# Attention and bilinear feed-forward block: the raw query weights land in XT3's place, and later tiles and PSUM banks take other places

## The chip, the cores and the metric

The kernel runs on one core of one Trainium2 chip. The metric is the device time of one execution in microseconds (us), the median of several runs. A profile is one further execution; its span goes from the first to the last instruction.

## What is computed

One transformer block on 2048 tokens of width 576, in float32:

```python
# 32 query heads of width 18, one shared key head and one shared value head
h  = x + softmax(q k^T / sqrt(18)) v @ wo        # q, k, v from layernorm(x) @ wq, wk, wv
h2 = h + ((n @ w_gate) * (n @ w_up)) @ w_down    # n = layernorm(h); 4608 hidden columns
```

## The kernel before

The tokens are worked in four blocks of 512 (`NB` = 4). Matrix products keep their precision by splitting one or both operands into a high part and a remainder, so a product is two or three matmuls.

**The opening** is `keys_values`. It loads the tokens and the raw weights, normalises each block, turns it over with TensorE transposes (`turns`), and splits the result into the tile `XT[b]` (`parts`: ScalarE writes the high part, VectorE the remainder). From `XT[b]` come the keys (`project`, `keys`), the values and, for block 0, the queries (`query`). The raw query weights come as four pieces of seven heads, `wqr0` to `wqr3`. ScalarE or GpSimd writes their high part to `wq_h` (`highs`, L276), GpSimd the remainder to `wq_l` (`lows`, L279); nothing reads a raw piece after that. The last piece is split by `highs(3, pool.tensor_copy)` and `lows(3)`, and the last block is written to `XT[3]` by the `parts()` behind `turns(3)`. `scale` works out the factors of the normalisation for some chunks of 128 tokens, and leaves minus mean times factor in a small tile `n` (L183).

**The rest.** After the opening, attention of block 0 runs with the queries of blocks 1 to 3 between (`queries`, L445). From about 360 us on the feed-forward of a block (`ffn`, gate and up products at L986, down products in `down` at L946) runs with the attention of a later block between its matmuls: `pair` issues scores (L593) and exponentials (L594), `flush` the sums over the values (L598). From about 1822 us only the last feed-forward work is left.

**What sets the order.** The order of each engine's instructions is the order in which the code issues them (`manual_schedule`). A tile pool gives every tile a place in SBUF (SBUF tiles of one tag share `bufs` slots, as large as the largest tile of the tag), and the layer below adds the semaphore waits that the slots need: who writes to a slot waits for the readers of the tile that was there. The pools lie one behind the other, in the order in which they are opened: `const`, `ln`, `resid`, `q`, `P`, `o`, `oT`, `w0`, then `p0q` (`wq_h`, `wq_l`, `kvq`, `XT0` to `XT3`) and `qb`; after the opening `w`, `hid` and `P2` take the room of `p0q` and `qb`. PSUM has eight banks: tag `s` has four of them (two tiles of two), `f` two, `m` and `a` one each, given out in the order in which the tags are first used.

Before the change the pieces `wqr1` to `wqr3` stand in the three slots of tag `wo_r` of pool `w0` (L145), which the output weights `wo_r` of block 0 use much later (`load_wo_0`, L714 to L716). The first tile in PSUM is `warm` of tag `a` (L305), into which 24 transposes run while the first tokens come in.

Of the kernel before, what the change touches and what calls it, by code (L numbers as in the profile page):

```python
# [17 lines left out]
F32 = mybir.dt.float32  # L18
F32R = mybir.dt.float32r
# [6 lines left out]
P = 128  # L26
S, D, H, DH, F = 2048, 576, 32, 18, 4608
TB = 512
NB = S // TB
NQ = TB // P  # L30
# [24 lines left out]
class Block:  # L55
# [78 lines left out]
    def keys_values(self, others):  # L134
# [7 lines left out]
        wkr = self.qp.tile([P, 5, 6 * DH], F32, tag="q", name="wkr")  # L142
        cols = [(slice(None), slice(None), slice(h0 * DH, (h0 + n) * DH)) for h0, n in QT]
        wqr = [self.qp.tile([P, 5, 7 * DH], F32, tag="q", name="wqr0")]
        wqr += [self.w0.tile([P, 5, 7 * DH], F32, tag="wo_r", bufs=3, name=f"wqr{i}") for i in range(1, 4)]  # L145
        for lo, hi in ((0, 1), (1, 2), (2, 4)):
            sp.dma_start(xs[0][:, lo:hi], self.tokens(self.x, 0)[:, lo:hi])
        sp.dma_start(self.C, self.cst)
# [8 lines left out]
        n = 5 * 6 * DH  # L157
# [17 lines left out]

        def scale(lo, hi, eng):
            r = self.rstd(mv[:, lo:hi, 1], f"a{lo}", eng, hi - lo)
            n = self.lp.tile([P, hi - lo], F32, tag=f"n{hi - lo}", name=f"n{lo}")
            if eng is pool:
                pool.tensor_tensor(n, mv[:, lo:hi, 0], r, ALU.mult)  # L180
                pool.tensor_scalar(n, n, -1.0, None, ALU.mult)
            else:
                dve.scalar_tensor_tensor(n, mv[:, lo:hi, 0], -1.0, r, ALU.mult, ALU.mult)  # L183
            for j in range(lo, hi):
                rs[j] = r[:, j - lo:j - lo + 1], n[:, j - lo:j - lo + 1]
# [33 lines left out]
        def parts(n=3):  # L219

            for _ in range(n):
                b, r, tr = trs.pop(0)
                XT = self.XT[b]
                if r is None:
                    self.split_tail(XT[:, 8, :], tr)
                else:
                    sl = slice(2 * r * P, (2 * r + 2) * P)
                    self.split(XT[:, 0:4, sl], XT[:, 4:8, sl], tr)

        def project(b):  # L230
            psk = psks[b] = (self.ps_a if b < 2 else self.ps_m if b == NB - 1 else self.ps_f)(f"psk{b}")
            for i, (w, m) in enumerate(highs_first(w_h, w_l, self.XT[b])):
                pe.matmul(psk[:6 * DH], w, m, start=(i == 0), stop=(i == 13))
# [47 lines left out]
        def query(i):  # L281
            psq = psqs[i] = self.ps_f(f"psq0_{i}")
            for k, (w, m) in enumerate(highs_first(self.wq_h[cols[i]], self.wq_l[cols[i]], self.XT[0])):
                pe.matmul(psq[:7 * DH], w, m, start=(k == 0), stop=(k == 13))
                yield
# [16 lines left out]
            self.flush(len(self.pend) - 1)  # L302

        q0, q1, q2, q3 = (query(i) for i in range(4))
        warm = self.ps_a("warm")  # L305
        for _ in range(WARM):
            pe.transpose(warm[:, 0:P], self.ident, self.ident)
        stats(0, 4)
        highs(0, act.copy)
        highs(1, act.copy)  # L310
        scale(0, 4, dve)
        apply(0, 0, 1, on=dve)
        apply(0, 2, 3)
        act.copy(w_h, wkr)
        turns(0)
        stats(4, 6)
        parts()
        pool.tensor_tensor(w_l, wkr, f32(w_h), ALU.subtract)
        lows(0)
        lows(1)  # L320
        highs(2, act.copy)
        lows(2)
        stats(6, 8)
        scale(4, 8, pool)
        drain(project(0))
        mean()
# [25 lines left out]
        some(t1)  # L352
        stats(11, 12)
        scale(8, 12, pool)
        highs(3, pool.tensor_copy)
        lows(3)
        values(0, 4)
        turns(1)
        parts()
        stats(12, 14)  # L360
        scale(12, 14, pool)
# [10 lines left out]
        some(q3, 6)  # L372
        turns(2)
        parts()
        some(k1)
        some(q3, 4)
# [59 lines left out]
    def queries(self, b):  # L436

        pe, act, dve, sp = self.pe, self.act, self.dve, self.sp
        for i, (h0, n) in enumerate(QT):
            r = n * DH  # L440
            psq, psr = self.ps_f(f"psq{b}_{i}"), self.ps_f(f"psr{b}_{i}")
            w_h, w_l = self.wq_h[:, :, h0 * DH:h0 * DH + r], self.wq_l[:, :, h0 * DH:h0 * DH + r]
            for k, (w, m) in enumerate(passes(w_h, w_l, self.XT[b])):
                for o, ps in ((0, psq), (64, psr)):
# [266 lines left out]

    def load_wo_0(self, c):

        w = self.w0.tile([P, 5, 7 * DH], F32, tag="wo_r", bufs=3, name=f"wo_r{c}")  # L714
        r = self.wo_r0[c] = w.rearrange("p a b -> p (a b)")[:, 0:D]
        self.sp.dma_start(r, self.wo0[:, c])  # L716

    def split_wo_0(self):
# [437 lines left out]
    def run(self):  # L1156
        from contextlib import ExitStack
        tc = self.tc
        self.q_dram = tc.dram_tile([NB, H * DH, 3, TB], F32, name="q_dram")
        self.wd_dram = tc.dram_tile([NC, P, 7, 2, HD], F32, name="wd_dram")  # L1160
        self.m_dram = tc.dram_tile([NB, 2, H, TB], F32, name="m_dram")
        self.known, self.n_mx = [0] * NB, 0
        self.tqs, self.p2 = [], None
        self.begin(True)
        with ExitStack() as st:
            pool = lambda name, bufs, **k: st.enter_context(tc.tile_pool(name=name, bufs=bufs, **k))
            cp, self.lp, self.hp = pool("const", 1), pool("ln", 2), pool("resid", 2)
            self.qp, self.pp, self.op, self.otp = pool("q", 2), pool("P", P_BUFS), pool("o", 1), pool("oT", 1)
            self.ps, self.w0 = pool("ps", 1, space=PSUM), pool("w0", 3)
            self.C = cp.tile([P, C_W], F32, name="C")  # L1170
            self.ident = self.C[:, C_ID:C_ID + P]
            self.kT = cp.tile([P, S], F32R, name="kT")
            self.V = cp.tile([P, NT, 32], F32, name="V")
            self.G = cp.tile([P, 64], F32R, name="G")
            self.mx = cp.tile([H, 8], F32, name="mx")
            st.enter_context(tc.manual_schedule())
            with tc.tile_pool(name="p0q", bufs=1) as self.p0q:
                self.wq_h = self.p0q.tile([P, 5, 28 * DH], F32R, name="wq_h")
                self.wq_l = self.p0q.tile([P, 5, 28 * DH], F32R, name="wq_l")
                self.kvq = self.p0q.tile([P, NB, TB], F32, name="kvq")  # L1180
                self.XT = [self.p0q.tile([P, 9, TB], F32R, tag=f"XT{b}", name=f"XT{b}") for b in range(NB)]
                with tc.tile_pool(name="qb", bufs=2) as self.qb:
                    def rest():
                        for b in range(1, NB):
                            yield from self.queries(b)
                    others = rest()
                    self.keys_values(others)
                    self.cast = self.dve.tensor_copy
                    live, due = True, 0.0
                    while live:  # L1190
                        if self.n_pair >= WO_FROM and not self.wo_r0:
                            for c in range(3):
                                self.load_wo_0(c)
                        self.pair()
                        due += RATE
                        while due > 0 and live:
                            z = next(others, None)
                            live = z is not None
                            due -= z or 0
                        self.pair()  # L1200
                        self.run_aux(1)
                        self.flush(len(self.pend) - 1)
            self.wp, self.hh, self.p2 = pool("w", 2), pool("hid", 4), pool("P2", 1)
            self.blocks()
            self.guard()
# [43 lines left out]
def passes(W, Wl, XT):  # L1249

    r = []
    for c in range(4):
        r += [(W[:, c], XT[:, c]), (W[:, c], XT[:, 4 + c]), (Wl[:, c], XT[:, c])]
    return r + [(W[:, 4], XT[:, 8]), (Wl[:, 4], XT[:, 8])]


def highs_first(W, Wl, XT):

    p = passes(W, Wl, XT)
    return p[0:12:3] + p[2:12:3] + p[1:12:3] + p[12:]  # L1260
# [86 lines left out]
```

## Time and profile before

| what | value |
|---|---|
| median of 3 runs | 2292.12 us (2291.93 to 2294.34) |
| the profiled execution's own time | 2291.9 us |
| its span | 2290.4 us |
| mean granted TensorE clock | 0.999 |
| TensorE (PE) busy | 2268.7 us |
| VectorE (DVE) busy | 1180.3 us |
| ScalarE (ACT) busy | 1436.5 us |
| GpSimd (POOL) busy | 681.3 us |

PE is TensorE's matmuls, PEld its weight loads, which run beside them. An engine's name with a q behind it (SPq, DVEq) is its sequencer: DMA issues and instructions that only wait. In a row of a group, "385/392/502" is the shortest, the median and the longest duration in ns; "fp32r" is the float32 form that the fast matmuls take. In a row of the timeline the first number is the start in us, the second the length of the piece, and what stands in brackets is how long the engine sat idle before and what ended that.

### The profile page before, as it was taken

Reading aid. Unit: us, or ns where it says so; the run is one execution under the profiler, and the core shown is the slowest. Engines: PE = TensorE matmul, PEld = TensorE weight load, DVE = VectorE, ACT = ScalarE, POOL = GpSimd, SP = SyncE. Lnnn points to the kernel's source line nnn. Section 1 sums busy time; section 2 is a strip of 40 time slices with the busy share of each in tenths; the row PEclk is TensorE's granted clock in tenths of the full one; section 3 lists DMA queues with packets and bytes.
Section 4 is the critical chain, followed back from the end, with each engine's and each line's share of the span. In section 5 each row is a group of like instructions: output and inputs, shape, how many; then the busy total and the mean of one; then the engine's idle time right before and its main releaser. Section 6 shows DMA issues by size and latency. Waiting matters only on the chain.

```text
span 2290.4 us, 45926 instructions
## 1 busy us (share of the span) xinstructions
PE 2268.7 (99%) x18114; PEld 1599.6 (70%) x18114; DVE 1180.3 (52%) x2152; ACT 1436.5 (63%) x1877; POOL 681.3 (30%) x856
## 2 busy tenths in 40 slices
PE   8999999999999999999999999999999999999998
PEld 6333346677777767677767677777767788888987
DVE  8232435565656567343434355444444476566665
ACT  5889887776676666767666767667677623232332
POOL 4000003455554444122221222222122233333342
PEclk9999999999999999999999999999999999999999
DMA  5222304434333344533333343633333354655553
GB/s 176 81 75 73 111 30 136 148 139 151 136 122 128 136 159 137 207 115 122 113 114 105 125 128 125 192 125 120 98 118 118 120 173 171 213 171 171 179 186 109
DMA packets 127129, 306.75 MB, mean 134 GB/s; under 512 B 17553, under 2 KB 17681, under 8 KB 126265
## 3 DMA queue, kind: packets, MB, share of 16 engines
q1 hardware_dynamic: 126905, 303.73, 39.8%
q8 instruction: 145, 2.38, 0.4%
q14 instruction: 79, 0.65, 0.1%
HBM read 233.76 MB, written 55.67 MB: 126 GB/s over the span
## 4 chain that ended last, share of the span: by engine, by line


## 5 line engine op out<-in xcount | busy, mean ns | idle before, releaser
L594 ACT ACTIVATE P<-s 128x1024 f32<-128x1024 f32 x1024 | 1024.0, 1026 | 271.4 <-PE s L593 189.6
L986 PE MATMUL pg<-X,ws 64*128 64x512 f32 x2592 | 706.9, 391 | 0.0
L986 PE MATMUL pu<-X,ws 64*128 64x512 f32 x2592 | 706.7, 391 | 0.1
L986 PEld LDWEIGHTS pg<-X,ws 64*128 64x128 f32 x2592 | 480.2, 186 | 75.9 <-issue 1.2
L986 PEld LDWEIGHTS pu<-X,ws 64*128 64x128 f32 x2592 | 478.1, 186 | 19.1 <-DVE h L751 1.0
L598 PE MATMUL acc<-P,V 128*32 128x512 f32 x4096 | 487.9, 598 | 0.0
L593 PE MATMUL s<-q,kT 56*128 56x512 f32 x2048 | 455.3, 423 | 5.2 <-ACT P L594 3.3
L946 PEld LDWEIGHTS y<-wdo,room 128*128 128x128 f32 x2856 | 386.9, 188 | 46.7 <-issue 44.2
L946 PE MATMUL y<-wdo,room 128*128 128x288 f32 x2856 | 403.7, 300 | 0.0
L953 ACT COPY tmp<-y 128x288 f32<-128x288 f32 x408 | 162.7, 399 | 330.8 <-PE y L946 313.2
L593 PEld LDWEIGHTS s<-q,kT 56*128 56x128 f32 x2048 | 208.1, 184 | 199.4 <-ACT P L594 118.3
L986 PE MATMUL gu<-X,ws 64*128 64x512 f32 x2592 | 301.8, 389 | 0.5 <-DMA X<-X 0.5
L954 POOL TENSOR_TENSOR x<-x,tmp 128x288 f32<-128x288 f32 x204 | 159.1, 810 | 446.2 <-ACT tmp L953 445.7
L598 PEld LDWEIGHTS acc<-P,V 128*32 128x32 f32 x4096 | 114.0, 109 | 242.5 <-issue 231.1
L986 PEld LDWEIGHTS gu<-X,ws 64*128 64x128 f32 x2592 | 247.6, 184 | 48.8 <-issue 4.8
L88 POOL CAST ws<-wr 128x1152 fp32r<-128x1152 f32 x144 | 170.9, 1187 | 325.6 <-PE pu L986 176.2
L954 POOL TENSOR_TENSOR h<-h,tmp 128x288 f32<-128x288 f32 x204 | 159.1, 810 | 345.8 <-ACT tmp L953 345.6
L89 DVE TENSOR_TENSOR ws<-wr,ws 128x1152 fp32r<-128x1152 f32 x144 | 199.1, 1383 | 74.7 <-POOL ws L88 74.7
L1020 DVE TENSOR_TENSOR hf<-pu,g 128x512 f32<-128x512 f32 x96 | 66.3, 691 | 269.0 <-ACT g L1016 265.6
L949 DVE TENSOR_TENSOR x<-x,y 128x288 f32<-128x288 f32 x272 | 117.7, 452 | 145.6 <-PE y L946 145.6
L949 DVE TENSOR_TENSOR h<-h,y 128x288 f32<-128x288 f32 x272 | 118.4, 454 | 111.8 <-PE y L946 109.8
L89 DVE TENSOR_TENSOR room<-S,room 128x1024 fp32r<-128x1024 f32 x68 | 85.1, 1251 | 147.7 <-ACT room L88 147.7
(172 smaller groups left out, 1621.9 us busy)
## 6 DMA issues: line engine op xcount, KB each, us to landing
wdo<-wd_dram SPq DMA_DIRECT2D x369, 288.0 KB
wr<-in_wgu_dram SPq DMA_DIRECT2D x144, 576.0 KB
wd_dram<-wdo SPq DMA_DIRECT2D x123, 288.0 KB
q<-q_dram SPq DMA_DIRECT2D x64, 216.0 KB
raw<-in_wd_dram SPq DMA_DIRECT2D x36, 288.0 KB
q_dram<-qs SPq DMA_DIRECT2D x15, 504.0 KB
X<-X SPq DMA_DIRECT2D x24, 256.0 KB
ob<-ob SPq DMA_DIRECT2D x121, 36.0 KB
```

Of the source, the lines that this page charges most:

```text
L88: (copy or self.cast)(hi, src)
L89: self.dve.tensor_tensor(lo, src, f32(hi), ALU.subtract)
L593: self.pe.matmul(s_[:, i], self.kT[o:o + 56, t * P:(t + 1) * P], q[o:o + 56, pr], start=True, stop=True)
L594: self.act.activation(p_, s_, AF.Exp, scale=SCALE)
L598: self.pe.matmul(acc[32 * j:32 * j + 32, :], self.V[:, t, :], Ps[j // 2][:, j % 2, :], start=(t == 0), stop=(t == NT - 1), skip_group_chec ...
L946: pe.matmul(y[:, :HD], m[:, t * P:(t + 1) * P], k, start=(first and j == 0), stop=(j == 2), skip_group_check=True)
L949: dve.tensor_tensor(hs, hs, y[:, :HD], ALU.add)
L953: act.copy(z, y[:, :HD])
L954: pool.tensor_tensor(hs, hs, z, ALU.add)
L986: pe.matmul(ps, w[o:o + 64, wk, c], X[o:o + 64, xk, c], start=(j == 0), stop=(j == 26))
L1020: dve.tensor_tensor(hf, pu, g, ALU.mult)
```

## The change

Four edits:

1. `wqr1` to `wqr3` become three parts of one tile `wqr` with the tag `XT3` in pool `p0q`, and the tile `XT3` itself is made when `parts` first needs it, in the same slot.
2. `wo_r` tiles have 576 columns and no longer 630.
3. The tiles `n` of two and four columns share one tag of two slots; before they had two tags of two slots each.
4. `warm` is a tile of tag `m` and no longer of tag `a`.

```diff
-        wqr += [self.w0.tile([P, 5, 7 * DH], F32, tag="wo_r", bufs=3, name=f"wqr{i}") for i in range(1, 4)]
+        late = self.p0q.tile([P, 3, 5, 7 * DH], F32, tag="XT3", name="wqr")
+        wqr += [late[:, i] for i in range(3)]
...
-            n = self.lp.tile([P, hi - lo], F32, tag=f"n{hi - lo}", name=f"n{lo}")
+            n = self.lp.tile([P, NQ], F32, tag="n", name=f"n{lo}")[:, :hi - lo]
...
                 b, r, tr = trs.pop(0)
+                if b == len(self.XT):
+                    self.XT.append(self.p0q.tile([P, 9, TB], F32R, tag=f"XT{b}", name=f"XT{b}"))
                 XT = self.XT[b]
...
-        warm = self.ps_a("warm")
+        warm = self.ps_m("warm")
...
-        w = self.w0.tile([P, 5, 7 * DH], F32, tag="wo_r", bufs=3, name=f"wo_r{c}")
-        r = self.wo_r0[c] = w.rearrange("p a b -> p (a b)")[:, 0:D]
+        r = self.wo_r0[c] = self.w0.tile([P, D], F32, tag="wo_r", bufs=3, name=f"wo_r{c}")
...
-                self.XT = [self.p0q.tile([P, 9, TB], F32R, tag=f"XT{b}", name=f"XT{b}") for b in range(NB)]
+                self.XT = [self.p0q.tile([P, 9, TB], F32R, tag=f"XT{b}", name=f"XT{b}") for b in range(NB - 1)]
```

In the built programs every engine has the same computing instructions and DMAs in the same order, with the same shapes. Two things differ.

**Places.** Byte offsets within a partition, and banks, as the two programs have them:

| tiles | before | after | moved by |
|---|---|---|---|
| `C`, `kT`, `V`, `G` (pool `const`) | from 1152 | the same | 0 |
| residuals, `q`, `P`, `ob`, `os`, `oT`/`room` | e.g. `q` 32064, `room` 77536 | 32000, 77472 | -64 |
| `wq_h`, `XT0`, `X`, `ws`, `wr`, `wdo`, `hf`, `P2` (all pools behind `w0`) | e.g. `X` 103552, `ws` 149632 | 102816, 148896 | -736 |
| `wqr1`, `wqr2`, `wqr3` | 95968, 101024, 98496 | 186464, 188984, 191504 | |
| PSUM tag `a` (the sums `acc`) | bank 0 | bank 5 | |
| PSUM tag `m` (every third `y`, and others) | bank 5 | bank 0 | |

The 64 bytes are the two small slots of edit 3, the other 672 the three narrower slots of edit 2. The offsets of the third row are multiples of 64 before, and 32 past a multiple of 64 after; a shift of 64 changes nothing in that respect.

**Waits.** On ScalarE and VectorE the first writes of the last block's turned tokens, and a tile `n`, wait for one more engine or queue. The rows name, behind the instruction, the semaphores that it waits for. ScalarE at the end of the opening, where the last block (tiles `tr`, `trt`) is written to `XT3` (its rows have the number 103 before and 691 after); first before the change:

```order
L248 COPY kvq<-psk_638 108x512
L88 CAST XT_103<-tr_0_659 128x4x256 [waits PE_49]
L88 CAST XT_103<-tr_1_668 128x4x256 [waits PE_49]
L97 CAST XT_103<-trt_677 128x512 [waits PE_49]
L594 ACTIVATE P_0_2_0_720<-s_0_2_0_719 128x1024 [waits PE_49]
```

and the same place after it:

```order
L251 COPY kvq<-psk_635 108x512
L88 CAST XT_691<-tr_0_656 128x4x256 [waits DMAHW1_49,PE_49,Pool_49]
L88 CAST XT_691<-tr_1_665 128x4x256 [waits PE_49]
L97 CAST XT_691<-trt_674 128x512 [waits PE_49]
L597 ACTIVATE P_0_2_0_718<-s_0_2_0_717 128x1024 [waits PE_49]
```

Nothing moved; the first of the three writes now also waits for GpSimd (`lows(3)`, the last reader of the raw weights) and for the queue of their last DMA. VectorE a little earlier, where the last factors are worked out (`ya`, `n`) and then the same tile is written; before:

```order
L124 SCALAR_TENSOR_TENSOR ya_601<-ta_600,ya_601 128x2 [waits DVE_49]
L183 SCALAR_TENSOR_TENSOR n_615<-mv,ya_601 128x2 [waits DVE_49]
L273 COPY V<-psv_632 128x4x18 [waits PE_49]
L192 TENSOR_SCALAR x_109<-x_109,mv,ya_468 128x576 [waits Pool_49]
L192 TENSOR_SCALAR x_109<-x_109,mv,ya_468 128x576
L425 SCALAR_TENSOR_TENSOR tq_7_388<-qs_1_385 126x512
L425 SCALAR_TENSOR_TENSOR tq_14_547<-qs_2_544 126x512
L251 TENSOR_REDUCE kabs<-kk_686 44x1 [waits Activation_49]
L253 SCALAR_TENSOR_TENSOR kk_686<-kvq,nmean,kk_686 44x512 [waits DMAHW4_49,DMAHW5_49,DMAHW3_49,Activation_49]
L89 TENSOR_TENSOR XT_103<-tr_0_659,XT_103 128x4x256 [waits Activation_49]
```

and after:

```order
L124 SCALAR_TENSOR_TENSOR ya_598<-ta_597,ya_598 128x2 [waits DVE_49]
L184 SCALAR_TENSOR_TENSOR n_612<-mv,ya_598 128x2 [waits DVE_49,Pool_49]
L276 COPY V<-psv_629 128x4x18 [waits PE_49]
L193 TENSOR_SCALAR x_108<-x_108,mv,ya_465 128x576 [waits Pool_49]
L193 TENSOR_SCALAR x_108<-x_108,mv,ya_465 128x576
L428 SCALAR_TENSOR_TENSOR tq_7_385<-qs_1_382 126x512
L428 SCALAR_TENSOR_TENSOR tq_14_544<-qs_2_541 126x512
L254 TENSOR_REDUCE kabs<-kk_683 44x1 [waits Activation_49]
L256 SCALAR_TENSOR_TENSOR kk_683<-kvq,nmean,kk_683 44x512 [waits DMAHW4_49,DMAHW5_49,DMAHW3_49,Activation_49]
L89 TENSOR_TENSOR XT_691<-tr_0_656,XT_691 128x4x256 [waits DMAHW1_49,Activation_49]
```

Again nothing moved. `n` waits for GpSimd, which wrote the tile that held the shared slot, and the first write of `XT3` for the DMA queue. Where an instruction has more waits than it can carry, the program puts an instruction that only waits (EVENT_SEMAPHORE) ahead of it: one more on ScalarE, two more on VectorE. On TensorE the first transpose into bank `m` (`trt`, L210) waits for the 24 transposes into `warm`, its own earlier instructions. On SP's queue the three loads of `wo_r` at about 270 us lose a wait for GpSimd, with three such instructions, and the load of the first `wr` gains one.

## The prediction

> **What bounds the kernel now.** I read the page's first two parts first, then the busy time by stage, then the groups of TensorE's lines. The page: busy time, busy tenths in 40 slices, granted clock in tenths.
>
> ```profile
> PE 2268.7 (99%) x18114; PEld 1599.6 (70%) x18114; DVE 1180.3 (52%) x2152; ACT 1436.5 (63%) x1877; POOL 681.3 (30%) x856
> ...
> PE   8999999999999999999999999999999999999998
> ...
> PEclk9999999999999999999999999999999999999999
> ```
>
> PE is busy in all but 2290.4 - 2268.7 = 21.7 us of the span, and the clock is granted in full. By stage (length, then busy time of each engine, clock, DMA share, GB/s; the opening up to 52 us, block 0's attention to 360, feed-forward beside attention to 1822, the last feed-forward):
>
> ```profile
> 0.00:36.00 36.00, 28.41 (x151) 23.27 (x153) 29.70 (x78) 14.90 (x22) 19.48 (x48) 1.00 0.71 233
> 36.00:52.00 16.00, 15.15 (x96) 10.76 (x94) 15.08 (x36) 12.13 (x16) 4.96 (x18) 1.00 0.26 88
> 52.00:360.00 308.00, 303.36 (x2145) 119.69 (x2145) 114.67 (x226) 263.74 (x278) 8.12 (x11) 1.00 0.22 71
> 360.00:1822.00 1462.00, 1460.93 (x11984) 1045.87 (x11980) 734.32 (x1306) 1004.88 (x1291) 481.52 (x585) 1.00 0.40 134
> 1822.00:2290.40 468.40, 460.83 (x3750) 399.99 (x3746) 286.50 (x509) 140.84 (x274) 167.16 (x195) 1.00 0.50 170
> ```
>
> In the long stage PE lacks 1.1 of 1462 us, while VectorE works half of it, ScalarE 69%, GpSimd 33% and the DMA engines 40%. A change that moves no instruction can thus act in two ways only: it makes a matmul longer, or it adds a wait ahead of PE in the opening, where PE idles 7.6 + 0.9 us. ScalarE, VectorE, GpSimd and DMAs have room for small losses in the long stage.
>
> **The new waits.** Each of the added semaphores was raised long before it is asked for. The timeline of the opening:
>
> ```profile
> 34.00 0.23 POOL L181 TENSOR_SCALAR n<-n 128x4 f32<-128x4 f32 x1
> 34.18 0.71 POOL L276 CAST wq_h<-wqr 128x630 fp32r<-128x630 f32 x1
> ...
> 34.98 1.48 POOL L279 TENSOR_TENSOR wq_l<-wqr,wq_h 128x630 fp32r<-128x630 f32 x1
> ...
> 36.46 0.75 PEld L284 LDWEIGHTS psq<-XT,wq_h 128*126 128x126 f32 x4 [0.37 <-POOL wq_l L279]
> ...
> 47.51 0.16 DVE L183 SCALAR_TENSOR_TENSOR n<-mv,ya 128x2 f32<-128x2 f32 x1
> ...
> 47.71 1.63 ACT L194 ACTIVATE x<-x,n,ya 128x576 f32<-128x576 f32 x2 [2.81 <-DVE n L183]
> ...
> 50.55 1.93 ACT L88 CAST XT<-tr 128x1024 fp32r<-128x1024 f32 x2
> ...
> 51.60 2.35 DVE L89 TENSOR_TENSOR XT<-tr,XT 128x1024 fp32r<-128x1024 f32 x2
> ```
>
> The tile `n` of 47.51 takes the slot whose last user on GpSimd ended at 34.00 + 0.23 = 34.23: 13.3 us of margin. The first write of XT3 on ScalarE, at 50.55, waits for the last reader of the raw weights, which ended at 34.98 + 1.48 = 36.46: 14.1 us of margin. Their DMA had landed by 34.18, where the cast reads them. The raw loads wait for nothing new. So no wait lasts; what stays is the waiting instruction itself. From the groups of three lines, the sequencers' own rows:
>
> ```profile
> L949 DVEq EVENT_SEMAPHORE  x136: 21/21/21, 401.0 to 2269.9; - x136
> ...
> L953 ACTq EVENT_SEMAPHORE  x401: 17/17/17, 401.4 to 2269.4; - x134
> ...
> L986 PEldq EVENT_SEMAPHORE  x32: 51/51/51, 495.0 to 2255.6; - x32
> ```
>
> Two more on VectorE cost 2 x 21 = 42 ns, one on ScalarE 17 ns, together 59 ns. They lie on the opening's path: ScalarE waited 2.81 us for that `n` (47.71), then normalises the chunks that the transposes read; behind the XT3 writes wait the next exponentials and, on VectorE, `qs` for the queries. TensorE's new wait in front of `trt` is for transposes that ended before 16 others; I cost it at nothing, and at most 51 ns if it acted like a waiting instruction. The three fewer and one more on SP's queue at 270 us issue loads of output and feed-forward weights; there GpSimd is what waits, off the path. Sum of the waits: +0.06 us, at most +0.11.
>
> **The raw weights' place.** GpSimd's two operations on the last piece are on the path: PE waited 0.37 us for their end. Three of the four pieces change their offset. All four give these rows:
>
> ```profile
> L279 POOL TENSOR_TENSOR wq_l<-wqr,wq_h x4: 1402/1451/1477, 14.1 to 35.0; 128x630 fp32r<-128x630 f32 x4
> ...
> L88 POOL CAST wos<-wor x15: 654/667/892, 466.2 to 1859.8; 128x576 fp32r<-128x576 f32 x15
> ...
> L88 POOL CAST wo<-wo_r x5: 662/667/1200, 274.7 to 284.0; 128x576 fp32r<-128x576 f32 x5
> ```
>
> The first spreads over 75 ns. The other two are one operation of one shape, from `wor`, which stands on a multiple of 64 bytes, and from `wo_r`, of which two slots in three do not: 667 ns both in the median. So I take nothing, with 0.08 us either way as bounds.
>
> **The later tiles' places.** Here lies all that could matter. X, ws, wq, wdo and XT move from a multiple of 64 bytes to 32 past one; q, P and the residuals keep their remainder by 64. TensorE's rows:
>
> ```profile
> L986 PE MATMUL pg<-X,ws x2592: 383/392/502, 359.4 to 1821.7; 64*128 64x512 f32 x200
> ...
> L986 PE MATMUL gu<-X,ws x2592: 383/386/502, 1825.9 to 2276.2; 64*128 64x512 f32 x200
> ...
> L445 PE MATMUL psq<-XT,wq_h x108: 385/392/498, 55.8 to 264.4; 64*126 64x512 f32 x108
> ...
> L946 PEld LDWEIGHTS y<-wdo,room x2856: 186/188/193, 396.3 to 2269.8; 128*128 128x128 f32 x191
> L946 PE MATMUL y<-wdo,room x2856: 290/297/404, 396.3 to 2269.9; 128*128 128x288 f32 x191
> ...
> L284 PEld LDWEIGHTS psq<-XT,wq_h x36: 184/186/189, 17.6 to 51.5; 128*126 128x126 f32 x36
> ```
>
> The weights of `y` come from `room`, which stands 32 past a multiple of 64 bytes before and after: 188 ns a load. Those of `psq` come from `wq_h`, on a multiple of 64: 186 ns, for two columns fewer. That is the operand that is loaded, and its loads run beside matmuls. The other operand, which streams (X, XT, wdo), starts on a multiple of 64 in every row of before, so the trace has no row for what comes. The nearest rows are one form from two tiles at different places: `pg` from X and `psq` from XT both take 392 ns in the median, `gu` from X 386. The 6 ns go with the stage and not with the place, since `pg` and `gu` read the same X. Between places the rows show no difference down to their last digit, so I take 0 and keep 1 ns either way as bounds. Gate and up matmuls are 7776 (pg, pu and gu, 2592 each), two at a time on half of the rows each, so 3888 stretches of PE's time; with the 2856 of `y` that makes 6744, and 1 ns each is 6.7 us.
>
> The Trainium skill, SBUF — State Buffer, section "Door 1: The DMA port swizzle", says that SBUF works in lines of 16 bytes, and that full speed needs two or more hits in each line. A shift of 736 = 46 x 16 bytes would leave the lines that a stream touches as many as before; by this rule the bounds of 6.7 us fall away and the time is 2292.2 us. The rows on `room` and `wo_r` agree with it; no run here shows it for a streamed operand.
>
> **Banks.** `acc` and every third `y` change banks 0 and 5. VectorE adds `y` from banks 5, 6 and 7 in turn:
>
> ```profile
> L949 DVE TENSOR_TENSOR h<-h,y x272: 453/454/456, 1500.9 to 2270.3; 128x288 f32<-128x288 f32 x136
> ```
>
> All within 3 ns, so a reader sees no bank. The matmuls into `acc` (bank 0 so far) are as even:
>
> ```profile
> L598 PE MATMUL acc<-P,V x4096: 592/592/617, 43.7 to 1825.3; 128*32 128x512 f32 x196
> ```
>
> I take nothing for the exchange; a gain or a loss of up to 1 ns in each of these 4096, which run four at a time, would be 1.0 us.
>
> **DMAs and the other engines.** Their tiles move too. What PE waited for a DMA behind the opening is the copies within X:
>
> ```profile
>   DMA X<-X: 2.1, 4
> ```
>
> If these copies became a tenth slower or faster, that would be 0.2 us; I take 0. VectorE, ScalarE and GpSimd have a third of the long stage and more to spare, so a few ns in each of their instructions hide there. If that cover were gone, a late exponential would show first, since PE's next scores wait for its tile; the rows of `room` say that ScalarE and VectorE write at 32 past a multiple of 64 all the time.
>
> **Sum.** Own time of the profiled execution 2291.9 us; waits +0.06; raw weights 0; places 0; banks 0; DMAs 0: 2291.96 us. The median of the runs shown is 0.2 us above that execution, so I forecast 2292.2 us. The terms' bounds are 6.7 + 1.0 + 0.2 + 0.1 us and nearly the same below, most of it the streamed operand's.
>
> **The rivals.**
>
> *Slower by place.* A stream that starts 32 bytes past a multiple of 64 takes an extra step, at 1 ns a stream: 6744 x 1 ns = 6.7 us, so 2298.9 us. It decides from 0.7 ns on (0.7 x 6744 = 4.7 us, 0.2%). For it: no row of before has such a stream, and 99% of the time is PE's, so nothing hides it. Against it: loads of weights and casts from such places take what they take elsewhere.
>
> *Faster by place.* Before, PE's streams may meet the accesses of other engines in the same part of the memory, and with X 672 bytes nearer to P they would meet less: minus 1 ns a stream, 2285.5 us. For it: `gu`, 386 ns, runs where ScalarE is busy 30% of the time (140.84 of 468.40 us) and `pg`, 392 ns, where it is 69%. Against it: the stages differ in much else (scores and sums stand between the matmuls of `pg`), and the sums over P are even to the ns at all places of P.
>
> *The new place of the raw weights is a bad one.* The change then costs in the opening instead of doing nothing. The longest row of GpSimd's cast is 1200 ns where the median is 667, a factor of 1.8; both operations on the last piece, 0.71 + 1.48 us, would take 1.8 us more, and PE already waits for them: 2294.0 us, still within 0.2%.
>
> *The change does not do what it says.* A wait for XT3's slot that lasts would show it: it decides only if `lows(3)` ended 14.1 us later than it does. With the same instructions ahead of it on GpSimd nothing in the trace leads there; I give it no chance of its own.
>
> **How the numbers follow.** Forecast, 2290.5 to 2294 us: 0.69. Bad place of the raw weights: 0.03. Slower by place: 0.14. Faster by place: 0.14. About 0.2%, 4.6 us, is what a measurement of this kernel can tell from no change; so within 0.2% has 0.69 + 0.03 = 0.72, faster and slower 0.14 each. The range takes in the bounds of the unknown term on both sides, 2285.5 to 2298.9 us, and leaves out only what goes beyond 1 ns a stream.
>
> **What would show it.** Right: medians of `pg` 392, `gu` 386, `y` 297 ns to within 1 ns, PE busy 2268.7 us to within 1 us, and the pieces from 50.55 us on starting less than 0.2 us later. Slower or faster by place: these medians, or the starts of one matmul after another, move by a ns or more in the stages from 360 us on, at the same idle time. A bad place in the opening: GpSimd's row of `wq_l` longer than 1477 ns. The prediction fails if one of the things that the rows cannot show (a streamed operand at such a place, PE's write to bank 5 beside a read of bank 4) costs more than 1 ns.

## The result, and the profile after the change

The changed kernel takes 2288.29 us (median of 13 runs, 2286.73 to 2289.22), the kernel before, on the same chip, 2293.46 us (13 runs, 2291.07 to 2294.46). The ratio is 0.9979, with a 95% interval of 0.9972 to 0.9986: **faster by 0.21%**, some 5 us. The profiled execution of the changed kernel took 2287.82 us, its span is 2286.0 us, 4.4 us shorter than before. Two executions of the later runs had a lower granted clock (0.85 in one of the kernel before, 0.63 in the profiled one of e11) and are left out of the ratios, and no steps are read for e11.

The page of the changed kernel, busy time of each engine:

```profile
PE 2262.5 (99%) x18114; PEld 1601.3 (70%) x18114; DVE 1183.7 (52%) x2152; ACT 1437.3 (63%) x1877; POOL 682.7 (30%) x856
```

TensorE has the same 18114 matmuls and is busy for 6.2 us less; VectorE is busy for 3.4 us more, GpSimd for 1.4 and ScalarE for 0.8. The changed kernel by stage, with the columns of the table in the prediction:

```profile
0.00:36.00 36.00, 26.84 (x146) 21.99 (x147) 28.60 (x77) 14.87 (x21) 18.40 (x47) 1.00 0.68 226
36.00:52.00 16.00, 15.06 (x94) 10.40 (x93) 15.12 (x36) 10.99 (x15) 6.02 (x19) 1.00 0.31 101
52.00:360.00 308.00, 303.60 (x2149) 119.97 (x2146) 115.85 (x228) 264.77 (x278) 8.16 (x11) 1.00 0.22 71
360.00:1822.00 1462.00, 1460.45 (x12025) 1051.01 (x12024) 740.93 (x1313) 1009.33 (x1295) 484.37 (x586) 1.00 0.42 134
1822.00:2286.00 464.00, 456.52 (x3712) 397.93 (x3708) 283.21 (x503) 137.39 (x269) 165.70 (x194) 1.00 0.51 171
```

Look at the counts, not at the busy times. In the long stage PE is as full as before (1460.45 of 1462 us), but starts 12025 matmuls in it where it started 11984. In the opening to 36 us it starts 146 where it started 151. So the opening loses a little, and the stage with attention gains more, though PE's idle time there did not shrink. The groups of TensorE's lines in the changed kernel (shortest, median and longest ns; first and last start in us):

```profile
L988 PE MATMUL pg<-X,ws x2592: 383/388/501, 359.9 to 1817.3; 64*128 64x512 f32 x200
L988 PE MATMUL gu<-X,ws x2592: 383/386/498, 1821.4 to 2272.0; 64*128 64x512 f32 x200
...
L948 PE MATMUL y<-wdo,room x2856: 288/295/402, 396.7 to 2265.8; 128*128 128x288 f32 x191
...
L601 PE MATMUL acc<-P,V x4096: 592/592/617, 44.8 to 1820.9; 128*32 128x512 f32 x196
```

The first and last starts show where the time came from. The first `pg` starts 0.5 us later than before (359.9, 359.4), the last 4.4 us earlier (1817.3, 1821.7): the stage with attention is 4.9 us shorter (1457.4, 1462.3). The `gu` matmuls behind it take 450.6 us from first to last, before 450.3: nothing gained. `pg` has a median of 388 ns where it had 392; `acc`, which changed its bank, is the same to the ns. `y` shows 295 for 297 ns, but two of its matmuls start 138.0 ns apart in the mean, before 138.2: of the 2 ns of duration 0.2 ns are time, 0.6 us over all 2856, in both stages together.

**What TensorE does in that stage.** Each gate matmul runs beside an up matmul on the other half of the rows, a *pair*. Three or four pairs stand between two pairs of scores. One such run in the timeline of the changed kernel (start and length in us):

```profile
1000.32 0.41 PE L596 MATMUL s<-q,kT 56*128 56x512 f32 x2
1000.55 0.39 PE L988 MATMUL pg<-X,ws 64*128 64x512 f32 x1
1000.57 0.39 PE L988 MATMUL pu<-X,ws 64*128 64x512 f32 x1
1000.78 0.39 PE L988 MATMUL pg<-X,ws 64*128 64x512 f32 x1
1000.79 0.39 PE L988 MATMUL pu<-X,ws 64*128 64x512 f32 x1
1001.00 0.39 PE L988 MATMUL pg<-X,ws 64*128 64x512 f32 x1
1001.02 0.39 PE L988 MATMUL pu<-X,ws 64*128 64x512 f32 x1
1001.23 0.39 PE L988 MATMUL pg<-X,ws 64*128 64x512 f32 x1
1001.25 0.39 PE L988 MATMUL pu<-X,ws 64*128 64x512 f32 x1
1001.47 0.41 PE L596 MATMUL s<-q,kT 56*128 56x512 f32 x2
```

A matmul lasts 390 ns, but the next pair starts 230 ns after the last, so the lengths say little. What counts is the **step**, from one pair's start to the next: here 0.23, 0.23, 0.22, 0.23, 0.24 us. A run of the kernel before:

```profile
1001.86 0.40 PE L593 MATMUL s<-q,kT 56*128 56x512 f32 x2
1002.09 0.39 PE L986 MATMUL pu<-X,ws 64*128 64x512 f32 x1
1002.10 0.39 PE L986 MATMUL pg<-X,ws 64*128 64x512 f32 x1
1002.32 0.39 PE L986 MATMUL pu<-X,ws 64*128 64x512 f32 x1
1002.34 0.39 PE L986 MATMUL pg<-X,ws 64*128 64x512 f32 x1
1002.56 0.39 PE L986 MATMUL pu<-X,ws 64*128 64x512 f32 x1
1002.57 0.39 PE L986 MATMUL pg<-X,ws 64*128 64x512 f32 x1
1002.79 0.39 PE L986 MATMUL pu<-X,ws 64*128 64x512 f32 x1
1002.79 0.39 PE L986 MATMUL pg<-X,ws 64*128 64x512 f32 x1
1003.02 0.40 PE L593 MATMUL s<-q,kT 56*128 56x512 f32 x2
```

Its steps are 0.23, 0.23, 0.24, 0.23, 0.23 us. One run is too coarse to tell the kernels apart. The table has the mean of each step by its place in the run, worked out from the starts of all matmuls between 360 and 1820 us:

| steps, ns | scores to 1st pair | 1st to 2nd | 2nd to 3rd | 3rd to 4th | 4th to scores | sum |
|---|---|---|---|---|---|---|
| before | 253.6 | 233.0 | 232.9 | 230.1 | 228.5 | 1178.1 |
| after | 251.1 | 229.7 | 227.3 | 227.2 | 234.8 | 1170.1 |

(The first step's mean holds a sixth of steps of some 335 ns before, and a fifth after; its median is 234 before and 229 after. How these long steps are counted moves the sum of a kernel by up to 5 ns and the 8.0 ns to anything from 6.9 to 8.1. The stage lengths do not depend on it.) Four steps are shorter and one is longer, 8.0 ns less for a run. The stage has 2592 pairs, so about 670 runs, and 8.0 x 670 = 5.4 us, where the stage is 4.9 us shorter. In the last stage there are no scores, and runs of mostly 54 pairs. There the steps fall to 226.7 ns within the first dozen pairs, before and after. So the short runs of the attention stage consist of steps that have not settled, and how long these steps are is what the change moved.

### The profile page after: what moved, and what is told of

Read it like the earlier page. It is cut to its first block, busy times and chain, and to the rows that moved or that the text cites. A ratio compares the mean times of both kernels' runs of the same rounds, so it can differ in the third digit from the quotient of the medians.

```text
span 2286.0 us, 45927 instructions
## 1 busy us (share of the span) xinstructions
PE 2262.5 (99%) x18114; PEld 1601.3 (70%) x18114; DVE 1183.7 (52%) x2152; ACT 1437.3 (63%) x1877; POOL 682.7 (30%) x856
## 4 chain that ended last, share of the span: by engine, by line
PE 94%; DVE 2%; DMA 1%; ACT 1%; issue 1%; SPq 0%; POOL 0%; ACTq 0%; DVEq 0%; POOLq 0%
PE pg L988 22%; PE acc L601 20%; PE y L948 17%; PE gu L988 13%; PE s L596 12%; PE pu L988 4%; PE yo L752 3%; PE psq L448 2%; DMA X<-X 1%; ACT P L597 1%; PE y L906 1%; DVE bsa L103 0%; DVE XT L89 0%; DMA x<-in_x_dram 0%; PE ye L906 0%
```

## The experiments

The order of the questions: which of the four edits, then which tiles, then by what rule. All ratios are to the kernel before, in runs on the same chip; its median there was 2293.0 to 2293.5 us.

### Banks or places

**e1_banks**: `warm` moved, nothing else.

```diff
-        warm = self.ps_a("warm")
+        warm = self.ps_m("warm")
```

> The kernel before with one edit alone: warm is a tile of tag m, so that acc and the third y exchange banks 0 and 5; no SBUF tile moves. Theory of the banks: all of the gain is here, about 2288.3 us (ratio 0.998), and the pairs of gate and up matmuls start 228 ns apart in the stage with attention (232 before, 228 after the change). Theory of the places: no difference from before, ratio 0.9995 to 1.0005, pairs 232 ns apart.

Measured: 2293.6 us, 1.0001 (0.9992 to 1.0010). The banks cost and bring nothing, and every step is within 0.2 ns of before (253.6, 232.8, 233.1, 230.0, 228.4).

**e2_places**: the change without its fourth edit.

```diff
-        warm = self.ps_m("warm")
+        warm = self.ps_a("warm")
```

> The changed kernel with warm back in tag a: all SBUF tiles stand at the new places, acc stays in bank 0 and the third y in bank 5. Theory of the places: the whole gain, ratio 0.998, pairs 228 ns apart in the stage with attention. Theory of the banks: no difference from before, 232 ns.

Measured: 2287.24 us, 0.9974 (0.9965 to 0.9984). The whole gain is there, with the steps of the change. So it comes from the tiles in SBUF. The next two took their two shifts apart.

**e3_small64**: the third edit alone. `q`, `P`, `X`, `ws` and all that lies behind `const` moves by -64 bytes.

```diff
-            n = self.lp.tile([P, hi - lo], F32, tag=f"n{hi - lo}", name=f"n{lo}")
+            n = self.lp.tile([P, NQ], F32, tag="n", name=f"n{lo}")[:, :hi - lo]
```

> The kernel before with one edit alone: the small tiles n share a tag, so that every tile behind them moves by -64 bytes and the remainder of each place by 64 stays. Theory of the remainder (32 past a multiple of 64 is what gains): no difference from before. Theory that any shift against kT and V (which stay) or by 256 matters: a gain or loss of up to 0.2%. Theory of the banks: no difference.

**e4_late672**: the first two edits alone. `X`, `ws` and all that lies behind `w0` moves by -672 bytes.

```diff
+        late = self.p0q.tile([P, 3, 5, 7 * DH], F32, tag="XT3", name="wqr")
...
+        r = self.wo_r0[c] = self.w0.tile([P, D], F32, tag="wo_r", bufs=3, name=f"wo_r{c}")
```

> The changed kernel without the shared small tag and with warm in tag a: only the pools behind w0 move, by -672 bytes, to 32 past a multiple of 64; q, P, the residuals and the banks stand as before. Theory of the remainder: the whole gain, ratio 0.998, pairs 228 ns apart. Theory of the banks: no difference. Theory that the 64 bytes of q and P are what matters: no difference.

Measured: e3 2288.33 us, 0.9980 (0.9971 to 0.9989); e4 2298.6 us, 1.0025 (1.0015 to 1.0035). The signs go apart. The small edit, which leaves every place's remainder by 64 as it was, gains as much as the whole change; the large one, which puts `X` and `ws` 32 bytes past a multiple of 64, loses alone and does not in the change. A rule by the remainder of a place is thereby out. The row of e3, then that of e4:

```profile
L986 PE MATMUL pg<-X,ws x2592: 384/387/501, 359.9 to 1817.0; 64*128 64x512 f32 x200
```

```profile
L988 PE MATMUL pg<-X,ws x2592: 383/393/502, 360.6 to 1827.8; 64*128 64x512 f32 x200
```

The stage with attention takes 1457.1 us in e3 and 1467.2 us in e4, with 1462.3 us before. The raw weights have the changed place in e4 and the old one in e3, so they are not the cause.

### Which tiles against which

Each of the next kernels moves a few tiles against the rest.

**e5_kT64**: `kT`, `V` and `G` move by +64, the rest stays. **e6_all64**: everything but `C` moves by +64 (the first two lines alone).

```diff
+            self.C = cp.tile([P, C_W + 16], F32, name="C")
...
+        sp.dma_start(self.C[:, 0:C_W], self.cst)
...
+            n = self.lp.tile([P, NQ], F32, tag="n", name=f"n{lo}")[:, :hi - lo]
```

> The kernel before with kT, V and G moved by +64 bytes and nothing else moved (C is 16 columns wider, and the shared small tag takes the 64 bytes back). Against kT, both q and X then stand 64 bytes lower, as in the run with the small tag alone. Theories: what counts is X against kT, or q against kT: the gain of that run, ratio 0.998, pairs of gate and up matmuls 229 ns apart in the stage with attention. What counts is the absolute place of X or q: ratio 1.000, 232 ns.

> The kernel before with all tiles except C moved by +64 bytes (C is 16 columns wider). No tile of the attention or feed-forward moves against another. Theories of X or q against kT: ratio 1.000, pairs 232 ns apart. Theory of the absolute place: a change of 0.1% or more either way.

Measured: e5 2289.39 us, 0.9984 (0.9975 to 0.9993); e6 2292.95 us, 0.9999 (0.9990 to 1.0008). Together they say that no tile has a good or bad place of its own, as far as a shift by 64 shows it. e6 moves all and has the steps of before (254.4, 233.0, 233.0, 230.1, 228.5); e5 moves the keys forward and gains nearly what e3 gained by moving the rest back. The row of e5, then that of e6:

```profile
L986 PE MATMUL pg<-X,ws x2592: 385/386/498, 361.6 to 1818.9; 64*128 64x512 f32 x200
```

```profile
L986 PE MATMUL pg<-X,ws x2592: 383/392/503, 361.4 to 1824.4; 64*128 64x512 f32 x200
```

From first to last these are 1457.3 and 1463.0 us, with 1462.3 before.

**e7_q64**: residuals, `q`, `P`, `ob` and `os` move by -64, `X` and `ws` stay. **e8_X64**: `room`, `X`, `ws` and what lies behind move by +64, `q` stays (the second line alone).

```diff
+            n = self.lp.tile([P, NQ], F32, tag="n", name=f"n{lo}")[:, :hi - lo]
...
-        rc = self.op.tile([P, TB // 32], F32, tag="rc", bufs=2, name=f"rc{b}_{g}")
+        rc = self.op.tile([P, TB // 32], F32, tag="rc", bufs=3, name=f"rc{b}_{g}")
```

> The kernel before with the residuals, q, P, ob and os moved by -64 bytes, and room, X, ws, wdo and the rest unmoved (the small tag is shared, and rc has a third slot, which gives the 64 bytes back behind it). Theory of q against kT: ratio 0.998, pairs 229 ns. Theory of X against kT: ratio 1.000, 232 ns. Theory of X against q: a change, of unknown sign.

> The kernel before with room, X, ws, wdo and all behind them moved by +64 bytes, and q, P and kT unmoved (rc has a third slot). Theory of q against kT: ratio 1.000, pairs 232 ns. Theory of X against kT: a change of 0.1% or more of unknown sign. Theory of X against q: the change of the run that moves q by -64, since X then stands at the same distance from q.

Measured: e7 2289.39 us, 0.9983 (0.9974 to 0.9992); e8 2292.49 us, 0.9997 (0.9988 to 1.0006). In total e8 looks like nothing, but its steps are others: 252.0, 236.6, 232.6, 231.0, 226.7. It loses 3.6 ns in the second step and gains in the first and the last. In both kernels `X` stands 64 bytes further from `q`, and only e7 gains, so that distance alone does not decide.

**e9_V64**: `V` and `G` alone move, by +64.

```diff
-            self.kT = cp.tile([P, S], F32R, name="kT")
+            self.kT = cp.tile([P, S + 16], F32R, name="kT")[:, 0:S]
...
+            n = self.lp.tile([P, NQ], F32, tag="n", name=f"n{lo}")[:, :hi - lo]
```

> The kernel before with V and G moved by +64 bytes alone (kT is 16 columns wider, the shared small tag takes the 64 bytes back behind them); q, P, X and kT stand where they stood. The run with kT, V and G at +64 gained 0.16%. Theory of q and X against kT: ratio 1.000, steps of gate and up pairs behind a pair of scores 233, 233, 230 ns as before. Theory of P against V: the gain is here, ratio 0.998.

Measured: 2293.94 us, 1.0004 (0.9995 to 1.0013), with the steps of before to within 0.3 ns. The values, moved by 64 against `P` and everything else, do nothing. So what is left of e5 is `kT`: loaded for the scores while `X` streams, and followed by `q`.

### By what rule

**e10_X160**: e4 with room added, so that `X` and `ws` move by -160, which is -672 + 512; `room` moves by +128. (Why 512: in the kernel the pieces of `ws` and `kT` that are loaded for one matmul lie 512 bytes apart, and the pieces of `X` and `q` that are streamed 2048. The distance between what is loaded and what is streamed thus changes from pair to pair, but its remainder by 512 is the same for all.)

```diff
-        rc = self.op.tile([P, TB // 32], F32, tag="rc", bufs=2, name=f"rc{b}_{g}")
+        rc = self.op.tile([P, TB // 32], F32, tag="rc", bufs=4, name=f"rc{b}_{g}")
...
+        r = self.wo_r0[c] = self.w0.tile([P, D + 32], F32, tag="wo_r", bufs=3, name=f"wo_r{c}")[:, 0:D]
```

> The kernel before with the raw weights in XT3's place and X, ws, wdo and the rest behind w0 at -160 bytes, which is -672 + 512 (wo_r tiles of 608 columns, rc with four slots; room +128). q, P, kT and V stand where they stood. Theory that only the place modulo 512 bytes counts: the loss of the run with -672, ratio 1.0025, steps 235, 233, 234 ns. Theory that the distance itself counts, or the part of the memory: another time, not predictable, 1.000 if nothing repeats.

Measured: 2299.05 us, 1.0023 (1.0013 to 1.0032), e4's time, and each step within 0.7 ns of e4's:

```profile
L988 PE MATMUL pg<-X,ws x2592: 383/393/501, 360.1 to 1827.6; 64*128 64x512 f32 x200
```

From 360.1 to 1827.6 are 1467.5 us; e4 had 1467.2.

**e11_kT2112**: `V` ahead of `kT` (the two lines exchanged), `C` 16 columns wider and the small tiles shared. `kT` moves by +2112 = 4 x 512 + 64, `V` to a place ahead of it, the rest stays as in e5.

> The kernel before with V ahead of kT: kT at +2112 bytes (2048 + 64), V at -8128 (-8192 + 64), C 16 columns wider, the small tag shared, so that q, P and X stand where they stood. Theory that only the place modulo 512 counts: as in the run with kT, V and G at +64, ratio 0.9984, steps 230, 229, 229 ns. Theory of the distance itself: another time and other steps.

Measured: 2288.24 us, 0.9978 (0.9969 to 0.9987), as e5 within the intervals. Only the time speaks here; the steps that were expected are not read.

**e12_kTback64**: `kT` 16 columns wider, so all behind it moves by +64. **e14_behind128**: 32 columns, +128.

```diff
-            self.kT = cp.tile([P, S], F32R, name="kT")
+            self.kT = cp.tile([P, S + 16], F32R, name="kT")[:, 0:S]
```

> The kernel before with everything behind kT moved by +64 bytes (kT is 16 columns wider): q and X stand 64 bytes higher against kT, the other way from the runs that gained. Theory of places that repeat, with no better and worse by themselves: a time that differs from before by 0.1% or more, of either sign, and steps unlike 233, 233, 230. Theory that a place 64 lower is simply better (some alignment): a loss, ratio 1.001 to 1.003.

> The kernel before with everything behind kT moved by +128 bytes. Plus 64 and minus 64 gave the same gain and the same steps, so I expect places to repeat every 128 bytes: ratio 1.000, steps 233, 233, 230 as before. Theory of a longer period (256 or 512): another time and other steps.

Measured: e12 2288.38 us, 0.9976 (0.9967 to 0.9985); e14 2295.18 us, 1.0008 (0.9999 to 1.0017). With +64 the same gain as with -64 (e3), step for step to within 1 ns; with +128 the steps of before but for the last, which is 231.7 for 228.5. So the distance of before is a bad one with good ones on both sides, and it nearly recurs after 128 bytes; after 512 it recurs wholly, as far as e10 and e11 show.

**e13_ws64**: `X` 16 elements longer, so `ws` and what lies behind move by +64 against `X`. Here the loaded weights are moved against the very stream that runs beside them.

```diff
+        n = 18 * TB
+        X = self.X = self.wp.tile([P, n + 16], F32R, tag="X", bufs=1, name=f"X{b}")[:, 0:n].rearrange("p (i c q) -> p i c q", i=2, c=9)
```

> The kernel before with ws, wr, wdo and all behind them moved by +64 bytes against X (the tile X is 16 elements longer); q, P, kT, V and X stand where they stood. Theory that a stream meets the weights that are loaded during it: the steps change where ws is loaded under q or under X (scores to pair, 234 ns in the median, and pair to pair, 233, 233, 230), the step from a pair to scores (227), where kT is loaded under X, stays; the time differs from before by 0.1% or more. Theory that only places against kT count: ratio 1.000, all steps as before.

Measured: 2305.5 us, 1.0056 (1.0042 to 1.0069), the largest effect of all. The rows of e13:

```profile
L987 PE MATMUL pg<-X,ws x2592: 386/391/498, 361.0 to 1828.1; 64*128 64x512 f32 x200
L987 PE MATMUL gu<-X,ws x2592: 385/391/502, 1832.2 to 2290.0; 64*128 64x512 f32 x200
```

It is the only kernel whose last stage changed clearly: `gu` takes 457.8 us from first to last where it took 450.3 (449.4 to 451.2 in all others that can be read), with a median of 391 for 386 ns. In that stage's long runs TensorE uses `X` and `ws` and nothing else. The steps there stay at 233.3 ns to the end of the run, where those of before, of the change and of e4 come down to 226.7. The stage has 1296 pairs: 1296 x 6.6 = 8.6 us by the settled steps, 7.5 measured.

e8, which moves both tiles by 64, settles at 226.7, so it is the distance between them. By the traces it does not depend on what else runs. Where VectorE, ScalarE and GpSimd stand still for at least 98% of a settled step, it takes 226.8 ns before (228 steps) and 233.3 in e13 (238 steps); where at every moment of it one of them works, 226.7 and 233.4. Where no DMA packet is under way, it takes 226.7 (445 steps) and 233.3 (466).

One part of the expectation failed: the step from a pair to the scores, where `kT` is loaded beside `X` and neither has moved, was to stay at its median of 227 ns. It rose to 233. So a step is not set by the two tiles at work in it alone; the pairs ahead of it count too.

**e17_q96_X64** and **e18_q32_X0**: an attempt to choose a good distance for each step: e4 with `kT` 24 columns wider (`q` +96, `X` -576) or 8 columns wider (`q` +32, `X` -640).

```diff
-            self.kT = cp.tile([P, S], F32R, name="kT")
+            self.kT = cp.tile([P, S + 24], F32R, name="kT")[:, 0:S]
```

> Raw weights in XT3's place, X and all behind w0 at -576 bytes, q and P at +96 against kT (by 128: q +96, X +64). Chosen from the steps: scores to pair took 229 ns in the median where X stood 32 less against q than before, and pair to scores 226 to 227 where X stood at 0 or 64 against kT; both hold here. Theory that the steps add up: faster than before by 0.3 to 0.5%, and faster than the change. Theory that the steps cannot be chosen apart: somewhere between 0.997 and 1.003.

> As the run before it, with q and P at +32 against kT and X at -640 (by 128: q +32, X 0). The same two conditions hold: X 32 less against q, X at 0 against kT. Theory that the steps add up: faster than before by 0.3 to 0.5%. Theory that they cannot be chosen apart: between 0.997 and 1.003.

Measured: e17 2293.56 us, 1.0003 (0.9994 to 1.0012); e18 2294.53 us, 1.0006 (0.9997 to 1.0015). In e17 the step from the last pair to the scores is the shortest of all, 225.8 ns, but the second step rose to 237.2, and the sum is that of before (1177.9). The row of e17:

```profile
L988 PE MATMUL pg<-X,ws x2592: 385/390/501, 359.7 to 1822.3; 64*128 64x512 f32 x200
```

The median duration, 390, would suggest a gain; the starts, 359.7 to 1822.3, say 1462.6 us, none. In e18 the step from the last pair to the scores is 232 ns in the median, where the expectation had 226 to 227. The steps of a run are not set one by one. That each carries on from how the last one ended would fit, but no run shows it. No version was found that beats the change by more than the intervals; e2 and e12 lie within it.

### All of them beside each other

Distances are moves against `kT` relative to before, in bytes; in brackets the same modulo 512, from -256 to 255. The stage is from the first `pg` to the last.

| kernel | `q` against `kT` | `X` against `kT` | stage, us | five steps, sum, ns | ratio |
|---|---|---|---|---|---|
| before, e1, e6, e9 | 0 | 0 | 1462.0 to 1463.0 | 1177.9 to 1179.0 | 0.9999 to 1.0004 |
| after, e2 | -64 | -736 (-224) | 1457.4, 1457.0 | 1170.1, 1169.8 | 0.9979, 0.9974 |
| e3, e5 | -64 | -64 | 1457.1, 1457.3 | 1169.8, 1171.3 | 0.9980, 0.9984 |
| e11 | -2112 (-64) | -2112 (-64) | | | 0.9978 |
| e12 | +64 | +64 | 1457.5 | 1170.2 | 0.9976 |
| e7 | -64 | 0 | 1458.6 | 1173.4 | 0.9983 |
| e8 | 0 | +64 | 1461.9 | 1178.9 | 0.9997 |
| e17 | +96 | -576 (-64) | 1462.6 | 1177.9 | 1.0003 |
| e18 | +32 | -640 (-128) | 1464.0 | 1181.6 | 1.0006 |
| e14 | +128 | +128 | 1464.2 | 1181.0 | 1.0008 |
| e4, e10 | 0 | -672, -160 (-160) | 1467.2, 1467.5 | 1187.8, 1188.0 | 1.0025, 1.0023 |
| e13 (`ws` +64 against `X`) | 0 | 0 | 1467.1 | 1186.4 | 1.0056 |

The stage follows the steps, to within what the counting of the long first steps leaves open, and the time follows the stage (e13 loses in the last stage too).

## Why the prediction was wrong

The forecast was 2292.2 us and no change that can be measured; the runs were faster by 0.21%. (It stood on a median of 2292.12 us for the kernel before, which took 2293.46 us in the runs beside the change.) By the prediction's own steps:

**The new waits (+0.06 us): right.** In the timeline of the changed kernel's opening:

```profile
7.19 0.82 DVE L103 BATCH_NORM_STATS2 bsa<-x 128x6 f32<-128x288 f32 x2 [1.56 <-DMA x<-in_x_dram]
...
36.11 1.48 POOL L282 TENSOR_TENSOR wq_l<-wqr,wq_h 128x630 fp32r<-128x630 f32 x1
...
48.72 0.16 DVE L184 SCALAR_TENSOR_TENSOR n<-mv,ya 128x2 f32<-128x2 f32 x1
...
48.91 1.63 ACT L195 ACTIVATE x<-x,n,ya 128x576 f32<-128x576 f32 x2 [2.89 <-DVE n L184]
...
51.75 1.94 ACT L88 CAST XT<-tr 128x1024 fp32r<-128x1024 f32 x2
```

The test that these pieces start less than 0.2 us later fails by its letter: the cast starts at 51.75 for 50.55. But the delay is there from the first tokens on: VectorE waits 1.56 us for their third piece (0.18 before), and `wq_l` starts 1.13 us later, ahead of any new wait. From there to the cast only 0.07 us are added. The kernel before got its third piece of tokens at 5.86 us in its profile, e1 and e6, which issue the same instructions there, at 8.00 and 8.05 us: this varies from run to run.

**The raw weights' place (0, 0.08 us either way): right.** Their row in the changed kernel has nearly the same durations as before; the longest, 1484 ns, is over the 1477 that the prediction named as a sign, but e1, with the weights at the old place, has 1497:

```profile
L282 POOL TENSOR_TENSOR wq_l<-wqr,wq_h x4: 1403/1434/1484, 15.4 to 36.1; 128x630 fp32r<-128x630 f32 x4
```

**Banks (0): right**, by e1 and by the unchanged row of `acc`. **DMAs and other engines (0): right** as far as PE's waits go, since PE's idle time did not shrink.

**The later tiles' places: this step failed.** It said "Between places the rows show no difference down to their last digit, so I take 0". It measured -4.9 us in the stage with attention. Ahead of it another 0.7 us went, where the 1.2 us of the late start became 0.5: from the cast above to the first `pg` it is 308.9 us before and 308.2 after. That part belongs to the first two edits, since it is 307.9 to 308.4 us in all six kernels that have them and 308.6 to 309.1 in the others (e11 not read); whether their places or their changed waits do it, no run separates. Four things were wrong in it. First, `q`, `P` and the residuals "keep their remainder by 64" was taken to mean that their move is harmless; e3, which changes no remainder, has the whole gain. Second, it compared one operand's place with another's, and asked whether a place is good. e6 shows that there is no such thing: all moved together is nothing. Third, "the 6 ns go with the stage and not with the place, since `pg` and `gu` read the same X" was half the reading. The stage has the scores in it, and with them `kT` and `q`; how much a run loses behind them depends on their places, and `pg` went to 388 where `gu` stayed at 386. Fourth, the bound of 1 ns a stream was too tight for a single step: by the table the steps moved by -5.6 to +6.3 ns and partly cancelled, and in e13 the settled step moved by 6.6 ns. It is by this luck that the total stayed inside the range. The tests named for this step showed it: PE busy fell by 6.2 us, and the starts moved in the stages from 360 us on.

**"Faster by place" had the sign and nearly the size** (-6.7 us bounded, about -5.2 measured), but not the mechanism, so the size is luck. It took PE's streams to meet the accesses of other engines. In the stage with attention the second to fifth steps beside which VectorE stands still take 232.7, 232.8, 230.3 and 228.3 ns before and 229.7, 227.5, 227.3 and 234.9 after, the same move as in the table; with GpSimd it is the same. ScalarE stands still beside enough steps only in the second one: 233.8 before (60 steps), 230.2 after (56). Two things stay possible there: a share of ScalarE, which writes `P` beside nearly all other steps, and one of VectorE in the first step, which (without the long ones) takes 239.8 ns before where VectorE works beside all of it and 234.8 where it stands still (229.0 and 228.4 after). For the last stage e13 leaves no room for other engines: the settled step is longer by as much where they stand still. e5 moves the keys, which only TensorE reads in this stage, and gains; e13 moves `X` and `ws` against each other and loses 12 us. All this fits TensorE's streamed operand against the weights that are loaded beside it. For `X` and `ws` in the long runs that is shown, for `kT` and `q` it is argued.

The Trainium skill, SBUF — State Buffer, section "Door 1: The DMA port swizzle", has lines of 16 bytes, and the prediction took from it that a shift by whole lines costs nothing. The runs disagree with that reading: e3 moves by 64 = 4 x 16 bytes and gains 0.20%, e13 moves one operand by 64 and loses 0.56%.

The Trainium skill, SBUF — State Buffer, section "Who interferes with whom", gives TensorE two read ports, one for the streamed operand and one for the weights, and calls them independent. By that, e13 should be as before; its settled step is 233.3 ns where it was 226.7.

**What stays open.** That distances between tiles decide, and not places, is shown by e3, e5 and e6; that one of them is the distance between what is streamed and what is loaded, by e13. That it recurs after 512 bytes is shown for two distances, e4 with e10 in every step and e5 with e11 in time alone. `q` was always moved together with `P` and the residuals; that it is `q` rests on TensorE not reading `P` in these runs. Why some distances settle in the long runs at 226.7 ns and one does not, why 64 bytes either way helped while 128 did not, and what in the memory or the array takes the time, no run here shows.

## What to carry to other kernels

In this kernel, which is 99% TensorE, where its tiles lie was worth from -0.3% to +0.6%, so in one like it an edit that resizes any tile, however small, needs a control: the same shift by a pad, without the edit. When a place is under suspicion, move it against each partner in turn and everything together once; a place that is judged alone tells nothing. Read such effects from the starts of successive matmuls in a stage and from the stage's length, since durations overlap, and their median pointed to a gain in e17 where there was none.

## What the runs showed of the hardware that was not expected

- A pair of 512-column matmuls on two row halves took from 225.8 to 237.2 ns from start to start (means of a place in the run, without the first), by nothing but the places of its operands and of those just ahead of it.
- Settling takes some seven pairs before and eleven after the change: in the last stage of before the steps from the second on go 231.8, 233.7, 228.5, 230.9, 229.0, 227.0 and end at 226.7 ns. With `ws` 64 bytes further from `X` they stay at 233.3.
- The exchange of two PSUM banks between sums that TensorE writes and VectorE reads did nothing: 1.0001 (0.9992 to 1.0010).
- The durations of `y` go with the place of `wdo` (295 ns in the change and in e4, 297 in e3 and before), while its starts stay 138.0 to 138.2 ns apart. Whether it is the place itself or the distance from `room`, no run separates.
